# A scan and a feed-forward network in one Trainium2 kernel: first unit's decays ahead of other prelude products, weight-decoding passes placed by step, and seven-product groups in another order

## The chip, the cores and the metric

The kernel runs on one core of a Trainium2 chip. The metric is the device time of one execution in microseconds (us), lower is better. Engines are named as in the profile: PE is TensorE's matmul pipe (PEld its weight loads), DVE is VectorE, ACT is ScalarE, POOL is GpSimd, SP is SyncE (SPq when it issues transfers).

## What is computed

The reference is a chunked linear-attention scan followed by a two-layer network without biases:

```python
log_a = np.log(np.clip(a, 1e-06, 1.0))          # a: 4 x 8 x 768
for each chunk:                                  # x: 4 x 8 x 768 x 32; B, C: 4 x 8 x 768 x 16
    cum = np.cumsum(la, axis=-1)
    L = np.exp(cum[..., :, None] - cum[..., None, :]) * causal
    y = (C @ B.T * L) @ x + (C @ state) * np.exp(cum)
    state = exp(sum(la)) * state + sum over j of B_j x_j * exp(cum_last - cum_j)
h = y.reshape(3072, 256) @ w_in                  # w_in: 256 x 2048
out = np.maximum(0.01 * h, h) @ w_out            # w_out: 2048 x 256
```

Everything is float32. The kernel takes the scan in chunks of 96 positions, which gives the same values.

## The kernel before

**Units of the scan.** A unit u is one chunk of one batch row with its 8 heads; there are 8 chunks of 4 batch rows, 32 units, in the order u = 4 * chunk + batch. Each unit needs a tile `lt` of decays (112 x 8 x 96), made in one of three ways. Units 0 and 1 (`DIRECT`) get theirs from two matmul groups: `decay_mask` writes the causal mask, `decay_direct` (L242) adds the sums, and `decay_of` (L272) takes the exponential on ACT. Units 2 to 15 use one matmul group, `decay_pe` (L261), on the operands `dl` and `dr`, into which `decay_load` brings split row sums by two transfers (L250, L253) from `parts_d` in HBM; `fill_slots` (L187) fills the constant rows. Units from 16 on use broadcast rows: a transfer (L279), a subtraction on POOL (`decay_sub`, L284), an exponential (L292) and a triangle select on POOL (L293). Then `scores` (L317, or L407 for two units at a time) multiplies C by B, DVE multiplies the scores into `lt` (L322 or L420), `unit_products` (L344, L353) makes the unit's output and next state, ACT copies the state (`stage`, L377) and the high half `xh` (L382), POOL spreads the state into the next chunk's `xs` (L380), and DVE subtracts the low half `xl` (L387). `state_decay` (L299) scales a chunk's B operand on POOL. Two groups, one for each unit, run behind each other in a loop of ten iterations u = 0 to 9 (`FIRST_UNITS`); iteration u issues `decay_pe(u + 2)`, `scores(u + 1)` and the products of unit u. Iteration 9 also issues the scores and multiplies of units 10 and 11 and the first network step. The other units come in pairs between network steps (`PAIR`, `STACKED_AT`, `STACKED_OUT`), by `pair_block` or `pair_now`.

**Weights.** There are 16 slices f of 128 hidden columns. Slice f arrives as 64-bit floats in `raw` (L96, 512 KB, three buffers) and is decoded: `decode_abs` on ACT (L441), then *passes* on DVE in a fixed queue: hold (L446), shift (L452), sign (L459), low (L466). After low, `defer` notes `decode_high` on ACT (L472, writes `wh`), `decode_abs` of slice f + 1, and for slices 0 to 3 the remainder `wl` on POOL (`rest_pool`, L512); for later slices the remainder is one more DVE pass (`decode_rest`, L479). What is deferred is issued by the next `settle`, which the loop calls once in each iteration or step (with `late=True` an entry waits one iteration more). `decode(n)` issues the next n passes. In `before` the prelude issues two passes, iterations 1 to 9 without 3 issue one each, and each network step issues `PASSES` = 2.

**Network steps.** There are six tiles t of 512 tokens. Tiles 0 to 3 go by steps s = (t, f) in the order of `CELLS`, 64 steps; a *cell* is a run of steps of one tile. `ffn_in(s)` is six matmuls of 512 columns (L550) into `hp`, of which there are two buffers; ACT makes `gh` (L557) and applies the activation in place (L560), DVE makes `gl` (L563) and so frees `hp`. `ffn_out(s)` (L574, six matmuls), `LAG` = 3 steps later, adds into the two output banks; at a cell's last step the banks are emptied by ACT and DVE (L586, L588) or, with an earlier partial result, by two DVE additions (L582). The next cell's first `ffn_out` needs the emptied banks, and its step is held back one step for that.

**Tiles 4 and 5** are done together at the end (`two_tiles`), with seven products in place of eight for each pair p of slices, eight periods p. One period issues on PE: products into the banks A, B and C, a slot, `product(A, False, a12, ...)`, `product(B, False, s3, ...)`, a slot, `product(B, False, a22, ...)`, `product(C, False, s4, ...)`, and two slots. A product is three matmuls (L792); a slot is one earlier output group, six matmuls (L811, or L574 for the last steps of tile 3). On DVE: u2 = B + kept (L865), u3 = B + kept (L872), c22 = C + u3 (L873), c21 (L879), c12 (L880) and four `low` subtractions (L824); `kept` is ACT's copy of A. `sums` (L743, L752) and `sums_split` (L758) prepare the next period's weight sums on POOL. `product(B, ..., s3)` has to wait until u2 has read B, and the products after the second slot wait for c22.

**Order.** The schedule is manual: each engine runs its instructions in the order in which the code issues them.

Of the kernel before, what the change touches and what calls it, by code (L numbers as in the profile page):

```python
# [18 lines left out]
Q = 96  # L19
NC = S // Q  # L20
QE = Q + N
# [5 lines left out]
TS = 512  # L27
NT = NTOK // TS
B_COLS = NB * QE
LAG = 3  # L30
WARM = 6
WARM2 = 2
RAWS = 3
SHIFT = 448
# [20 lines left out]
LAST_OUT = 54  # L55
COMBINE = 56

PASSES = 2
KD = Q + 3 * NH + 3
MAG_MIN = float(np.uint32(0x38000000).view(np.float32))  # L60
MAG_MAX = float(np.uint32(0x47EFFFFF).view(np.float32))
# [3 lines left out]
def scan_ffn(ctx: ExitStack, tc: tile.TileContext, a_l, b_l, c_l, bn_l, x_l, w_l, out_l):  # L65
# [112 lines left out]
    def fill_first():  # L178
        nc.vector.tensor_copy(dr[:Q, 0], later.unsqueeze(1).to_broadcast([Q, NH, Q]))
# [64 lines left out]
                start=False, stop=True,  # L244
            )

    def decay_load(u, n):
        p, b = u * NH, (u - DIRECT) % SLOTS
        rows = parts_d[p:p + n * NH]
        nc.sync.dma_start(  # L250
            dl[Q:Q + 3 * NH, b:b + n, :Q], rows.rearrange("(u h) t i -> (h t) u i", h=NH)
        )
        nc.sync.dma_start(  # L253
            dr[Q + 3 * NH:KD, b:b + n].rearrange("t b h i -> t (b h) i"),
            rows.rearrange("r t i -> t r i"),
        )
# [336 lines left out]
    with tc.tile_pool(name="ps_d", bufs=2, space=PSUM, reuse_waits="tile") as ps_d:  # L593

        def free_tile():
            return ps_d.tile([128, 2, TS], F32, name="pd")

        nc.vector.tensor_scalar(
            out=la, in0=la, scalar1=1e-6, scalar2=1.0, op0=ALU.max, op1=ALU.min,
        )  # L600
        nc.scalar.activation(la, la, AF.Ln)
        pds = [free_tile() for _ in range(2)]
        second = score_tile()
        for u in range(DIRECT):
            fill_reach(u)
        nc.gpsimd.memset(ccs[1], 0.0)
        nc.vector.memset(dl[Q:], 1.0)
        nc.vector.memset(dl[Q:Q + 3 * NH, :, Q:], 0.0)
        fill_first()
        prow = first[:, 0, :Q]  # L610
        sum_rows(prow, 0)
        split_sums(prow)
        nc.sync.dma_start(parts_d, parts)
        fetch_w(0)
        decay_load(DIRECT, 2)
        decay_load(DIRECT + 2, SLOTS - 2)
        columns(erev, after, AF.Exp, second[:, 0])
        fill_less()
        for u in range(DIRECT):
            decay_mask(pds[u])  # L620
        keep_warm(second[:, 1], WARM2)
        state_decay(0)
        nc.scalar.copy(dl[:Q], upto_b.unsqueeze(1).to_broadcast([Q, SLOTS, QE]))
        fill_slots(1, SLOTS // 2)
        fill_slots(SLOTS // 2, SLOTS)
        decay_direct(0, pds[0])
        decay_of(0, pds[0])
        decode_abs(0)
        fetch_bc(1)
        fetch_bn(1)  # L630
        fetch_x(1)
        fetch_w(1)
        scores(0)
        decode(2)
        decay_direct(1, pds[1])
        decay_of(1, pds[1])
        for u in range(FIRST_UNITS):
            v = u + 2
            if u:
                decay_pe(v, free_tile())  # L640
            if u == 0:
                rest = unit_out(u, free_tile())
                rest()
            if u + 1 < FIRST_UNITS:
                scores(u + 1, int(0 < u < 4))
            else:
                pair_now((), (u + 1, u + 2))
                settle()
                pg = ctx.enter_context(tc.tile_pool(name="pg", bufs=LAG + 2))
                ffn_in(0, free_tile()[:, 0])  # L650
            if u:
                rest = unit_out(u, free_tile())
                rest()
            else:
                pd = free_tile()
                keep_warm(pd[:, 0], WARM2)
                decay_pe(v, pd)
            c, b = divmod(u, NB)
            if c + 2 <= 3:
                if b == 0 and c:  # L660
                    alloc_x(c + 2)
                    fetch_x(c + 2)
                if b == 2:
                    fetch_bc(c + 2)
                if b == 3:
                    fetch_bn(c + 2)
            if u == 3:
                fetch_x(2)
            if u == 4:
                fetch_w(2)  # L670
            if b == 2 and c < 2:
                state_decay(c + 1)
            if u > 7:
                fetch_more()
            if u:
                settle(late=True)
                if u != 3:
                    decode(1)
        ffn_act(0)
        ffn_low(0)  # L680

# [112 lines left out]
                skip_group_check=True,  # L794
            )

    def keep_out(t, m, op, half):
        ob = pob.tile([128, TS], F32, name=f"ob{m}")
        if half:
            nc.scalar.copy(ob[:, :TS // 2], op[:, :TS // 2])  # L800
            nc.vector.tensor_copy(ob[:, TS // 2:], op[:, TS // 2:])
        elif m == 0:
            nc.scalar.copy(ob, op)
        else:
            nc.vector.tensor_copy(ob, op)
        nc.sync.dma_start(out_l[m, :, t * TS:(t + 1) * TS], ob)

    def two_out(f, t, gh, gl, first, last):
        for m in range(2):
            for i, (half, x) in enumerate(((0, gh), (1, gh), (0, gl))):  # L810
                nc.tensor.matmul(  # L811
                    outs[t][m], lhsT=w_half[half][:, f, DM + m * 128:DM + (m + 1) * 128], rhs=x,
                    start=first and i == 0, stop=last and i == 2,
                )
        if last:
            for m in range(2):
                keep_out(t, m, outs[t][m], t == NT - 1 and m == 1)

    def act_split(h, gh, in_place):
        nc.scalar.activation(gh, h, AF.Prelu, alpha=0.01)  # L820
# [10 lines left out]
    def two_tiles(queue, pair, rhs):  # L831
# [9 lines left out]
        def slot():  # L841
            if queue:
                f = queue.popleft()
                f()
                if f is opens:
                    slot()

        for p in range(NP):
            f1, f2 = 2 * p, 2 * p + 1
            k1, k2 = slice(0, 128), slice(128, 256)  # L850
# [12 lines left out]
            product(C, True, s1, rhs["t1"])  # L863
            nc.scalar.copy(kept, A)
            nc.vector.tensor_tensor(out=u2, in0=B, in1=kept, op=ALU.add)  # L865
            if p + 1 < NP:
                sums(p + 1)
            slot()
            product(A, False, a12, rhs["21"])
            act_split(A, g["11"][0], A)  # L870
            product(B, False, s3, rhs["t3"])
            nc.vector.tensor_tensor(out=u3, in0=B, in1=kept, op=ALU.add)  # L872
            nc.vector.tensor_tensor(out=c22, in0=C, in1=u3, op=ALU.add)  # L873
            low(g["11"][1], A, g["11"][0])
# [9 lines left out]
            act_split(c21, g["21"][0], c21)  # L884
            low(g["21"][1], c21, g["21"][0])
            act_split(c12, g["12"][0], c12)
            low(g["12"][1], c12, g["12"][0])
            slot()
            slot()
            order = ("11", "21", "22", "12") if p == NP - 1 else ("11", "22", "21", "12")  # L890
# [10 lines left out]
    for s in range(total):  # L901
# [11 lines left out]
        settle()  # L913
        if late:
            late[1](0)
        if s:
            ffn_low(s)
        if late:
            late[1](1)
        late = None  # L920
        if s in stacked_at:
            u = stacked_at[s]
# [2 lines left out]
            for rest in rests:  # L925
                rest()
            late = (u + 1, mults)
        if s in pair_at:
            pair_now(*pair_at[s])
        decode(PASSES)  # L930
        if s == COMBINE:
            open_two()
            sums(0)
# [7 lines left out]
        if s == HELD_OUT:  # L941
            open_outs_pool()
        elif rested or not outs_due or steps[outs_due[0]] not in firsts or outs_due[0] == 0:
            while outs_due:
                ffn_out(outs_due.popleft())
            rested = False
        else:
            rested = True
    for _ in combining:
        pass  # L950
    assert not outs_due
# [42 lines left out]
```

## Time and profile before

| | us |
|---|---|
| median of three runs (lowest to highest) | 324.87 (323.07 to 325.5) |
| the profiled execution, its own time | 324.14 |
| its span, first to last instruction | 322.4 |
| PE busy, of the span | 311.1 |
| DVE busy | 213.4 |
| ACT busy | 181.4 |
| POOL busy | 132.5 |

The profiled execution's time is 1.74 us above its span; that part lies outside the instructions. PE's busy time overlaps between pipelined matmuls (a 512-column matmul shows about 390 ns, and they start 227 ns apart), so 96% is not a measure of what is left. The chain of waits follows the work that ended last backwards and is the better guide: where a row of it is not PE's, PE stood still.

### The profile page before, as it was taken

Reading aid. Unit: us, or ns where it says so; the run is one execution under the profiler, and the core shown is the slowest. Engines: PE = TensorE matmul, PEld = TensorE weight load, DVE = VectorE, ACT = ScalarE, POOL = GpSimd, SP = SyncE. Lnnn points to the kernel's source line nnn. Section 1 sums busy time; section 2 is a strip of 40 time slices with the busy share of each in tenths; the row PEclk is TensorE's granted clock in tenths of the full one; section 3 lists DMA queues with packets and bytes.
Section 4 is the critical chain, followed back from the end, with each engine's and each line's share of the span. In section 5 each row is a group of like instructions: output and inputs, shape, how many; then the busy total and the mean of one; then the engine's idle time right before and its main releaser. Section 6 shows DMA issues by size and latency. Waiting matters only on the chain.

```text
span 322.4 us, 6284 instructions
## 1 busy us (share of the span) xinstructions
PE 311.1 (96%) x2407; PEld 244.9 (76%) x2407; DVE 213.4 (66%) x349; ACT 181.4 (56%) x354; POOL 132.5 (41%) x216
## 2 busy tenths in 40 slices
PE   8999989999998999999999999999999999999995
PEld 4567768788886888788888877888877778777873
DVE  6788895797889797952634452296387577657561
ACT  5677775857575555545363534574366445644551
POOL 6388672613454443523434520070064356435100
PEclk9999999999999999999999999999999999999999
DMA  6777641462529240330213101000000000000003
GB/s 193 229 237 268 181 153 65 150 199 75 144 69 276 70 152 0 118 101 2 88 47 107 65 1 67 0 2 0 0 33 35 0 0 0 2 0 2 0 2 130
DMA packets 11722, 26.29 MB, mean 82 GB/s; under 512 B 2380, under 2 KB 4652, under 8 KB 11692
## 3 DMA queue, kind: packets, MB, share of 16 engines
q1 hardware_dynamic: 11692, 25.89, 25.3%
q8 instruction: 19, 0.31, 0.4%
q14 instruction: 11, 0.09, 0.1%
HBM read 22.57 MB, written 3.32 MB: 80 GB/s over the span
## 4 chain that ended last, share of the span: by engine, by line
PE 83%; DVE 8%; ACT 3%; issue 3%; DMA 2%; SPq 0%; ACTq 0%
PE op L574 26%; PE hp L550 24%; PE sc L792 9%; PE sc L811 6%; PE op L811 4%; PE hp L792 3%; PE sc L407 3%; PE sc L344 3%; DVE c L873 2%; DVE u L872 2%; PE sc L317 1%; PE pd L344 1%; PE pd L261 1%; DMA raw<-w_l 1%; DVE gl L563 1%
## 5 line engine op out<-in xcount | busy, mean ns | idle before, releaser
L563 DVE TENSOR_TENSOR gl<-hp,gh 128x512 fp32r<-128x512 f32 x63 | 43.4, 689 | 58.6 <-ACT hp L560 58.3
L557 ACT ACTIVATE gh<-hp 128x512 fp32r<-128x512 f32 x63 | 37.6, 597 | 63.7 <-PE hp L550 63.7
L574 PE MATMUL op<-gh,wh 128*128 128x512 f32 x128 | 51.0, 398 | 1.1 <-DVE ob L582 1.1
L550 PE MATMUL hp<-xh,wh 128*128 128x512 f32 x126 | 49.8, 395 | 0.4 <-DVE gl L563 0.4
L574 PE MATMUL op<-gh,wl 128*128 128x512 f32 x128 | 49.9, 390 | 0.0
L574 PE MATMUL op<-gl,wh 128*128 128x512 f32 x128 | 49.9, 390 | 0.0
L550 PE MATMUL hp<-xh,wl 128*128 128x512 f32 x126 | 49.1, 389 | 0.0
L550 PE MATMUL hp<-xl,wh 128*128 128x512 f32 x126 | 49.0, 389 | 0.0
L380 POOL COPY xs<-stage 16x64 f32<-16x64 f32 x112 | 31.6, 282 | 31.4 <-ACT stage L377 26.9
L758 POOL TENSOR_TENSOR sl<-s,sh 128x512 fp32r<-128x512 f32 x8 | 10.4, 1296 | 73.1 <-ACT sh L757 73.1
L293 POOL TENSOR_SCALAR_AFFINE_SELECT lt<-lt 96x768 f32<-96x768 f32 x16 | 15.1, 943 | 55.8 <-ACT lt L292 55.8
L560 ACT ACTIVATE hp<-hp 128x512 f32<-128x512 f32 x63 | 37.4, 594 | 0.0
L574 PEld LDWEIGHTS op<-gh,wh 128*128 128x128 f32 x128 | 24.0, 188 | 8.0 <-ACT gh L557 1.7
L550 PEld LDWEIGHTS hp<-xh,wh 128*128 128x128 f32 x126 | 23.7, 188 | 6.0 <-DVE gl L563 0.9
L574 PEld LDWEIGHTS op<-gl,wh 128*128 128x128 f32 x128 | 24.0, 188 | 5.1
L574 PEld LDWEIGHTS op<-gh,wl 128*128 128x128 f32 x128 | 24.0, 188 | 4.7
L550 PEld LDWEIGHTS hp<-xl,wh 128*128 128x128 f32 x126 | 23.6, 188 | 4.9
L284 POOL TENSOR_TENSOR lt<-lt,ccol 112x768 f32<-112x768 f32 x16 | 25.9, 1620 | 3.4 <-DMA lt<-crow_d 2.7
L550 PEld LDWEIGHTS hp<-xh,wl 128*128 128x128 f32 x126 | 23.7, 188 | 4.7
L824 DVE TENSOR_TENSOR gl<-c,gh 128x512 fp32r<-128x512 f32 x24 | 24.3, 1032 | 1.4 <-ACT c L821 1.2
L420 DVE TENSOR_TENSOR lt<-sc,lt 112x384 f32<-112x384 f32 x44 | 21.6, 549 | 3.0 <-ACT xh L382 1.9
L820 ACT ACTIVATE gh<-c 128x512 fp32r<-128x512 f32 x24 | 15.0, 627 | 14.7 <-DVE c L873 9.1
(165 smaller groups left out, 609.7 us busy)
## 6 DMA issues: line engine op xcount, KB each, us to landing
raw<-w_l SPq DMA_DIRECT2D x16, 512.0 KB, 3.9
lt<-crow_d SPq DMA_DIRECT2D x16, 336.0 KB, 4.6
xs<-x_l SPq DMA_DIRECT2D x8, 384.0 KB
out_l<-ob SPq DMA_DIRECT2D x12, 256.0 KB, 2.0
bn<-bn_l SPq DMA_DIRECT2D x8, 231.0 KB, 3.4
bt<-b_l SPq DMA_DIRECT2D x8, 224.0 KB, 4.7
cc<-c_l SPq DMA_DIRECT2D x16, 96.0 KB, 3.9
la<-a_l SPq DMA_DIRECT2D x1, 96.0 KB
```

What stands on the lines that cost most here:

```text
L284: nc.gpsimd.tensor_tensor(out=lts[u], in0=lts[u], in1=ccol[:, u * NH:(u + 1) * NH].unsqueeze(2).to_broadcast([QE, NH, Q]), op=ALU.subtract,)
L293: nc.gpsimd.affine_select(out=lt[:Q], in_=lt[:Q], pattern=[[0, NH], [1, Q]], compare_op=ALU.is_ge, fill=0.0, base=0, channel_multiplier=-1,)
L380: nc.gpsimd.tensor_copy(to[:, :, hh], stage[hh * D:hh * D + N])
L420: nc.vector.tensor_tensor(out=heads, in0=spaces[half][:QE, :, 2 * Q * e:2 * Q * (e + 1)], in1=heads, op=ALU.mult,)
L550: nc.tensor.matmul(hp, lhsT=w_half[half][:, f, k * 128:(k + 1) * 128], rhs=x[t][:, k, :], start=(n == 0), stop=(n == 5),)
L557: nc.scalar.activation(ghs[s], hp, AF.Prelu, alpha=0.01)
L560: nc.scalar.activation(hps[s], hps[s], AF.Prelu, alpha=0.01)
L563: nc.vector.tensor_tensor(out=gls[s], in0=hps.pop(s), in1=ghs[s], op=ALU.subtract)
L574: nc.tensor.matmul(op, lhsT=w_half[half][:, f, DM + m * 128:DM + (m + 1) * 128], rhs=x, start=(first and i == 0), stop=(last and i == 2),)
L792: nc.tensor.matmul(bank, lhsT=w[h], rhs=x[g], start=start and i == 0, stop=i == 2, skip_group_check=True,)
L811: nc.tensor.matmul(outs[t][m], lhsT=w_half[half][:, f, DM + m * 128:DM + (m + 1) * 128], rhs=x, start=first and i == 0, stop=last and i == 2,)
L824: nc.vector.tensor_tensor(out=gl, in0=g, in1=gh, op=ALU.subtract)
```

## The change

- *Prelude.* Three warming matmuls (`WARM`) instead of six; the two masks are issued straight after them, before the row sums, and the later two warming matmuls are gone. `decay_direct(0)` and its exponential come right after the first column sums; then half the constant rows of `dr`, the scores of unit 0, `decay_direct(1)`, the copy into `dl`, the two row loads, and the exponential of unit 1, then the other half of the rows. The first load's second transfer (the rows of `dr`) is issued by ScalarE instead of SP.
- *Weights.* `fetch_w(1)` moves from the prelude to iteration 2, `fetch_w(2)` from iteration 4 to 6; `decode_abs(0)` moves from the prelude to iteration 1.
- *Passes.* Iterations 2 to 9 issue `LEAD` passes. Steps issue `EARLY` (0 to 3), none in `BUSY`, three in `LIGHT`, otherwise two; in steps 1 and 3 two more stand between the two multiplies of a unit. `ffn_low` of these steps moves behind the second multiply.
- *Step 4.* The block of units 14 and 15 moves from before the passes to the end of the step, behind the output groups.
- *Seven-product groups.* `product(B, False, s3, ...)` goes ahead of `product(A, False, a12, ...)`; the `low` of c12 is issued one period later, after u2.
- *Last outputs.* Tile 5's second half is copied whole by ACT and its first half by DVE; before, the second half was shared between ACT and DVE and the first went to ACT.

Where the first passes stand (f is the slice):

| | before | after |
|---|---|---|
| prelude | hold 0, shift 0 | none |
| iterations 1 to 9 | sign 0; low 0; none; hold 1; shift 1; sign 1; low 1; hold 2; shift 2 | none; hold 0 and shift 0; sign 0; low 0; none; hold 1 and shift 1; sign 1; low 1; hold 2 |
| steps 0 to 3 | sign 2, low 2; hold 3, shift 3; sign 3, low 3; hold 4, shift 4 | none; shift 2, sign 2, low 2; none; hold 3, shift 3, sign 3, low 3 |

```diff
-WARM = 6
+WARM = 3
-PASSES = 2
+LEAD = (2, 1, 1, 0, 2, 1, 1, 1)
+EARLY = (0, 1, 0, 2)
+BUSY = (17, 21, 25, 30, 34, 38, 42, 46, 50)
+LIGHT = (9, 11, 13, 14, 16)
...
-    def decay_load(u, n):
+    def decay_load(u, n, eng=nc.sync):
...
-        nc.sync.dma_start(
+        eng.dma_start(
             dr[Q + 3 * NH:KD, b:b + n].rearrange("t b h i -> t (b h) i"),
...
         fill_first()
+        for u in range(DIRECT):
+            decay_mask(pds[u])
         prow = first[:, 0, :Q]
         sum_rows(prow, 0)
         split_sums(prow)
         nc.sync.dma_start(parts_d, parts)
         fetch_w(0)
-        decay_load(DIRECT, 2)
-        decay_load(DIRECT + 2, SLOTS - 2)
         columns(erev, after, AF.Exp, second[:, 0])
         fill_less()
-        for u in range(DIRECT):
-            decay_mask(pds[u])
-        keep_warm(second[:, 1], WARM2)
         state_decay(0)
-        nc.scalar.copy(dl[:Q], upto_b.unsqueeze(1).to_broadcast([Q, SLOTS, QE]))
-        fill_slots(1, SLOTS // 2)
-        fill_slots(SLOTS // 2, SLOTS)
         decay_direct(0, pds[0])
         decay_of(0, pds[0])
-        decode_abs(0)
+        fill_slots(1, SLOTS // 2)
+        scores(0)
+        decay_direct(1, pds[1])
+        nc.scalar.copy(dl[:Q], upto_b.unsqueeze(1).to_broadcast([Q, SLOTS, QE]))
+        decay_load(DIRECT, 2, nc.scalar)
+        decay_load(DIRECT + 2, SLOTS - 2)
+        decay_of(1, pds[1])
+        fill_slots(SLOTS // 2, SLOTS)
         fetch_bc(1)
         fetch_bn(1)
         fetch_x(1)
-        fetch_w(1)
-        scores(0)
-        decode(2)
-        decay_direct(1, pds[1])
-        decay_of(1, pds[1])
...
-                if u != 3:
-                    decode(1)
+            if u == 1:
+                decode_abs(0)
+            if u > 1:
+                decode(LEAD[u - 2])
...
+        if m == 0 and t != NT - 1:
+            nc.scalar.copy(ob, op)
+        elif t != NT - 1:
+            nc.vector.tensor_copy(ob, op)
         elif m == 0:
+            nc.vector.tensor_copy(ob, op)
+        else:
             nc.scalar.copy(ob, op)
...
             nc.vector.tensor_tensor(out=u2, in0=B, in1=kept, op=ALU.add)
+            if low_due:
+                low(*low_due.pop())
             if p + 1 < NP:
                 sums(p + 1)
             slot()
+            product(B, False, s3, rhs["t3"])
             product(A, False, a12, rhs["21"])
             act_split(A, g["11"][0], A)
-            product(B, False, s3, rhs["t3"])
...
             act_split(c12, g["12"][0], c12)
-            low(g["12"][1], c12, g["12"][0])
+            low_due.append((g["12"][1], c12, g["12"][0]))
+            if p + 1 == NP:
+                low(*low_due.pop())
...
         if late:
             late[1](0)
+            decode(2)
+            late[1](1)
         if s:
             ffn_low(s)
-        if late:
-            late[1](1)
...
-        if s in pair_at:
+        if s in pair_at and s != STACKED_OUT:
             pair_now(*pair_at[s])
-        decode(PASSES)
+        decode(EARLY[s] if s < len(EARLY) else 0 if s in BUSY else 3 if s in LIGHT else 2)
...
+        if s == STACKED_OUT:
+            pair_now(*pair_at[s])
```

More of the change, by code (lines that the diff above doesn't have):

```diff
@@ L664, in scan_ffn @@
                     fetch_bc(c + 2)
+                    if c == 0:
+                        fetch_w(1)
                 if b == 3:
@@ L668, in scan_ffn @@
                 fetch_x(2)
-            if u == 4:
+            if u == 6:
                 fetch_w(2)
@@ L795, in product, with keep_out @@
             )
-    def keep_out(t, m, op, half):
+    def keep_out(t, m, op):
         ob = pob.tile([128, TS], F32, name=f"ob{m}")
-        if half:
-            nc.scalar.copy(ob[:, :TS // 2], op[:, :TS // 2])
-            nc.vector.tensor_copy(ob[:, TS // 2:], op[:, TS // 2:])
+        if m == 0 and t != NT - 1:
+            nc.scalar.copy(ob, op)
+        elif t != NT - 1:
+            nc.vector.tensor_copy(ob, op)
         elif m == 0:
+            nc.vector.tensor_copy(ob, op)
+        else:
             nc.scalar.copy(ob, op)
-        else:
-            nc.vector.tensor_copy(ob, op)
         nc.sync.dma_start(out_l[m, :, t * TS:(t + 1) * TS], ob)
@@ L816, in two_out @@
             for m in range(2):
-                keep_out(t, m, outs[t][m], t == NT - 1 and m == 1)
+                keep_out(t, m, outs[t][m])
     def act_split(h, gh, in_place):
@@ L846, in slot @@
                     slot()
+        low_due = []
         for p in range(NP):
```

## The prediction

> **What bounds the kernel now.** I read the page first, then the chain of waits from end to end, then PE's list of waits, and last the timeline around each place where the chain leaves PE.
>
> ```profile
> span 322.4 us, 6284 instructions
> ...
> PE 83%; DVE 8%; ACT 3%; issue 3%; DMA 2%; SPq 0%; ACTq 0%
> ```
>
> ```profile
> PE sc L344 <- DVE lt L420: 1.9, 2, 1.4
> ...
> PE op L574 <- DVE ob L582: 1.1, 1, 1.1
> PE pd L261 <- ACT lt L272: 0.8, 1, 0.8
> ...
> PE hp L550 <- DVE gl L563: 0.4, 1, 0.4
> ```
>
> PE is the bound; what can be gained is the time in which it stands. The list (total us, times, longest) names four places outside the end: steps 2 and 4 (L420: 0.5 and 1.4), a cell's end (L582: 1.1), iteration 5 (L272: 0.8) and one late `gl` (0.4). The seven-product part waits a little in each of its periods:
>
> ```profile
> 253.22 0.69 PE sc L792 x3
> 253.94 0.70 DVE u L872
> 254.67 0.70 DVE c L873
> 255.41 1.67 PE sc L792 x6
> ...
> 258.47 1.36 PE op L811 x6
> ...
> 263.91 0.69 PE sc L792 x3
> ```
>
> Six 512-column matmuls take 1.36 us, 0.227 each. From s3 at 253.22 to the next s3 at 263.91 is one period, 10.69 us, for 45 matmuls (seven products of 3, four slots of 6), which is 10.20. The 0.49 between them comes from s3, u3 and c22 in a row: the slot beside them covers 1.36 of their 1.5 and latencies, and the restart costs the rest.
>
> **Prelude, 1.7 us earlier.**
>
> ```profile
> 5.57 1.46 PE L242 MATMUL pd<-lt,after 96*112 96x384 f32 x4
> ...
> 5.95 2.45 DVE L187 COPY dr<-dr 120x2304 bf16<-120x2304 bf16 x2 [0.29 <-ACT dr L183]
> ...
> 7.80 0.37 SPq L250 DMA_DIRECT2D dl<-parts_d  x1
> ...
> 9.46 0.68 ACT L441 ACTIVATE w<-raw 128x512 f32<-128x512 f32 x1 [1.59 <-DMA raw<-w_l]
> ...
> 10.04 0.79 ACT L272 ACTIVATE lt<-pd 112x768 f32<-112x768 f32 x1
> ...
> 11.46 1.01 DVE L322 TENSOR_TENSOR lt<-sc,lt 112x384 f32<-112x384 f32 x2
> ...
> 13.04 0.54 PE L344 MATMUL pd<-lt,xs 96*32 96x96 f32 x16
> ```
>
> Here the wait is on ACT: unit 1's exponential (10.04) stands behind `decode_abs(0)`, which waits 1.59 for the first weights. After the change, unit 0's matmuls start about 1.1 earlier (4.5), its exponential ends near 6.8, when ACT is free of the `dr` rows. DVE fills half the rows (1.2 of the 2.45), multiplies unit 0 until 8.2 and fills the rest until 9.5. ACT copies into `dl`, issues the row transfer once `parts_d` has landed (SP could issue at 7.80; 0.3 for the issue, as a bound 0 to 0.6) and runs unit 1's exponential from 8.1 to 8.9. DVE is then the later one: `xl` of unit 0 until 9.9, multiply of unit 1 from 9.9 and not 11.46. PE's products of unit 1 go from 13.04 to about 11.3: 1.7. The loads are the bound below: should their small packets, which sit behind the weights that ended at 9.46, land only at 10.5, it is 1.0. Three warming matmuls and the masks fill the same time as six did, so the row sums start as before: nothing. Moving `fetch_w(1)` and `fetch_w(2)` costs nothing: iterations later than their issue by 4 us use them.
>
> **Iterations 1 to 5, 0.3 us gained.** `decode_abs(0)` (0.68) now stands between `xh` and the next exponential on ACT, which has some 0.3 of room there: 0.4 lost. Two passes in iteration 2, where there was one, lose 0.2. `decode_high(0)` and `decode_abs(1)` leave iteration 4, and with them the wait of 0.8 (0.9 with its restart): gained.
>
> **Iteration 6, 2.8 us lost.** The same two ACT instructions, the POOL remainder and now two passes come in iteration 6, which has a POOL instruction that iteration 4 had not: `state_decay(2)`.
>
> ```profile
> 15.57 0.21 ACT L377 COPY stage<-pd 128x64 f32<-128x64 f32 x1 [0.51 <-PE pd L353]
> ...
> 17.45 1.06 POOL L299 TENSOR_TENSOR bn<-bn,erev 112x512 f32<-112x512 f32 x1
> ...
> 19.32 0.21 ACT L377 COPY stage<-pd 128x64 f32<-128x64 f32 x1 [0.59 <-PE pd L353]
> ...
> 20.90 0.43 DVE L446 TENSOR_SCALAR w<-w 128x512 f32<-128x512 f32 x1 [0.76 <-ACT w L441]
> 20.91 1.54 POOL L512 TENSOR_TENSOR wl<-w,wh 128x512 fp32r<-128x512 f32 x1
> ...
> 24.30 0.68 DVE L459 SCALAR_TENSOR_TENSOR w<-raw,w 128x512 uint32<-128x512 uint32 x1
> ```
>
> ```profile
> 126.52 1.23 POOL L293 TENSOR_SCALAR_AFFINE_SELECT lt<-lt 96x768 f32<-96x768 f32 x1 [4.97 <-ACT lt L292]
> ...
> 127.05 2.69 DVE L466 SCALAR_TENSOR_TENSOR w<-raw,w 128x512 uint32<-128x512 uint32 x1
> ...
> 127.73 1.46 POOL L284 TENSOR_TENSOR lt<-lt,ccol 112x768 f32<-112x768 f32 x1
> ```
>
> The second fence shows how a pass behaves against POOL: L466, issued at 127.05 while L293 ran, did not get in between L293 and L284 and ended at 129.74, after both. In the first, POOL's L512 came 0.01 behind hold (L446) and lasted 1.54. So they exclude each other, and a waiting engine goes first when the other has a gap. Counted from T, the start of `stage` of unit 6: hold 1 comes at T + 1.58 (20.90 less 19.32), L299 at T + 1.88 (17.45 less 15.57). Shift 1 needs hold 1 and so leaves a gap at T + 2.0; L299 takes it (1.06), L512 follows at once (1.3), and shift 1 ends near T + 4.6. The multiply of unit 8, queued behind it on DVE, started in before at T + 1.34; it starts at T + 4.6 now. DVE then works without a pause through iterations 7 to 9 (two multiplies 1.0 each, three `xl` 0.36, sign 1 and low 1 at 0.7 as at 24.30, the multiplies of units 10 and 11 at 1.95, hold 2, `gl(0)`), and PE's `decay_pe(12)`, which waits for `gl(0)`, comes 2.8 later by this count than at before's distance from T.
>
> The Trainium skill (SBUF — State Buffer, "SBUF: two separate sides") says that DVE instructions with two SBUF inputs or in a two-port mode, and GpSimd's, share one pair of ports, held by whichever starts first for the whole instruction. It speaks against putting two passes beside POOL work, and the trace agrees (2.69 for L466). It does not say who is next: if shift 1 gets in between L299 and L512, only 1.1 is lost at first; that is the first rival.
>
> **Steps 0 to 6, 0.1 us gained.** Without passes in step 0 and with `gl` behind the second multiply, the multiplies of units 13 and 15 come 0.6 and 0.5 earlier, so the wait of 0.5 in step 2 goes; in step 4 PE runs two output groups (2.72) in place of its wait of 1.4. But both are given back. ACT's `decode_high(2)`, issued in step 2, waits for low 2, which DVE reaches only after shift 2, sign 2, two multiplies (1.0 each) and `gl(1)`; the unit copies and the exponential of unit 14 stand behind it, and `decay_pe(15)` comes 0.2 later than before. Low 3 now ends step 3 and not step 2: ACT's high, then POOL's remainder, which slice 3's step 5 needs:
>
> ```profile
> 44.29 1.28 POOL L512 TENSOR_TENSOR wl<-w,wh 128x512 fp32r<-128x512 f32 x1 [0.90 <-ACT wh L472]
> 44.86 0.54 PE L344 MATMUL sc<-lt,xs 112*32 112x96 f32 x16 [1.36 <-DVE lt L420]
> ```
>
> Before, that remainder was ready at 45.57, with 3 us to spare. After, low 3 ends near 46.8 on the same scale, the remainder near 48.8, and step 5's second matmul, which could start at 47.6, waits for it. Net 0.1, with 1.9 (no wait returns) and -0.6 as its ends.
>
> **Ends of cells, 1.6 us gained.**
>
> ```profile
> 101.32 1.79 POOL L284 TENSOR_TENSOR lt<-lt,ccol 112x768 f32<-112x768 f32 x1 [2.18 <-DMA lt<-crow_d]
> ...
> 101.70 1.96 DVE L459 SCALAR_TENSOR_TENSOR w<-raw,w 128x512 uint32<-128x512 uint32 x1
> ...
> 104.41 0.47 PE L574 MATMUL op<-gh,wh 128*128 128x512 f32 x1 [1.05 <-DVE ob L582]
> ```
>
> The additions that empty the banks in step 21 stand behind sign 11, which is slow beside L284. With no pass in step 21 they run at 101.2 and PE does not wait: 1.2 with the restart. The other wait (0.4, some 0.6 with its restart) is the 2.69 of L466 above, low 14 ahead of `gl(30)`. There hold 14 and shift 14 stand now, which can lose to the same two POOL instructions, but are shorter: 0.4 of 0.6. The three-pass steps lie where PE has output groups to run. Bounds 0 and 1.8.
>
> **Seven-product groups, 4.2 us gained.** With a12 behind s3, PE has 0.68 + 1.36 to do while u3 and c22 run, about 1.5: the 0.49 goes, eight times 3.9. What must now be early is u2, before s3:
>
> ```profile
> 258.33 3.37 DVE L824 TENSOR_TENSOR gl<-c,gh 128x512 fp32r<-128x512 f32 x3
> 258.53 1.75 POOL L743 TENSOR_TENSOR w<-wh,wl 128x512 f32<-128x512 f32 x1
> ...
> 261.96 0.69 DVE L865 TENSOR_TENSOR u<-sc,kept 128x512 f32<-128x512 f32 x1 [0.27 <-issue]
> ...
> 263.07 0.39 PE L792 MATMUL hp<-xh,wh 128*128 128x512 f32 x1
> ```
>
> u2 ended at 262.65; s3 would start where a12 does, at 263.07: 0.4 of cover. The third `low` (0.95 of the 3.37) leaves u2's front, so u2 moves up by up to 0.7. In the second period u2 stood behind an output copy, and s3 waited about 0.6 on it; of that 0.3 to 0.5 goes. Sum 4.2, bounds 3.0 and 4.4.
>
> **Tail, 0.2 us gained.**
>
> ```profile
> 317.98 0.59 ACT L803 COPY ob<-op 128x512 f32<-128x512 f32 x1 [1.45 <-PE op L811]
> ...
> 318.66 0.37 ACT L800 COPY ob<-op 128x256 f32<-128x256 f32 x1
> 319.06 0.42 DVE L801 COPY ob<-op 128x256 f32<-128x256 f32 x1 [1.81 <-ACT ob L800]
> ```
>
> The halves ran one behind the other until 319.48. A whole ACT copy, 0.59 as at 317.98, ends at 319.25. Bounds 0 and 0.3.
>
> **Sum.** 1.7 + 0.3 - 2.8 + 0.1 + 1.6 + 4.2 + 0.2 = 5.3. The profiled execution took 324.14, its span and 1.74 around it: 318.8. The shown median, 324.87, is 0.7 above that execution and the lowest run 1.1 below; the sum rests on the profiled one.
>
> **Rivals.** (1) Shift 1 gets in before L512, or sign 1 rather than shift 1 loses: `decay_pe(12)` loses 1.5 in place of 2.8, 317.5. For it: hold 1 came ahead of L512 at 20.90; against: L466 was passed over at 127.73. (2) POOL is behind or ahead and nothing collides: only the two ACT instructions cost, 0.6, and 316.6. Against: 0.3 between the two arrivals. (3) The passes make new waits in the steps: with low 15 in step 35 (32 before) more passes meet L284, and the 1.6 comes back as waits, with 0.7 more at step 5: 321.1. (4) Slower: DVE becomes the bound in the three-pass steps 9, 11, 13, 14 and 16. A step then has `gl` and three passes, 2.5 us, and with one pass held off by L284 as at 101.70 (1.3 more) 3.8, against 2.72 of PE's; `hp` comes free late and PE waits 1.0 in each, 5.0, on top of rival 3's 2.3: 324.14 - 5.3 + 7.3 = 326.1. It decides from a wait of 0.6 in each. For it: how long a pass is held off; against: `hp` has two buffers, so that a late `gl` is wanted a step later, and steps 10, 12 and 15 have two passes. (5) The prelude's gain is not there since the loads land late, 1.0 in place of 1.7: 319.5, inside the forecast's own spread.
>
> **Chances.** Forecast 0.47 (with 5), rival 1 0.2, rival 2 0.13, rival 3 0.17, rival 4 0.03. One per cent of the time before, 3.2 us, is about what a measurement of this kernel can tell from no change, so 321.6 is the border: rival 3 lies at it, and I give it half. Faster 0.88, within 0.1, slower 0.02. The range leaves out half of rival 3 and all of 4 above and the best of 2 below: 315.6 to 321.3.
>
> **What would show it.** Right: no row of u3 and c22 in the chain between 230 and 305, and 10.2 from s3 to s3; no wait on L582; unit 1's products near 11.3; a shift 1 of over 2 us near L299 and L512 in iteration 6; a wait of PE's step 5 for L512. The forecast is wrong if the first network step comes earlier than before by over 0.5 us (rival 1 or 2; by the forecast it comes about 0.8 later), if periods still take 10.6, or if PE waits for `gl` or `ob` in steps 9 to 40 for over 1 us (rival 3, and from 5 us rival 4).

## The result, and the profile after

The changed kernel took 325.68 us in the median of nine executions (319.15 to 327.12), the kernel before 324.54 in nine of the same comparison. The nine lie in three groups: one at 319.15, three at 321.6 to 322.2, five at 325.7 to 327.1. The comparison leaves the last five out as disturbed, which gives a ratio of 0.99 (95%: 0.9857 to 0.9942); since the upper group turns out to come from the clock at the kernel's start, all nine are kept here and told apart below. By the median of all nine the change gains nothing. One of the nine, 319.15, lies in the forecast's range of 315.6 to 321.3. The profiled execution is one of the middle group, 321.56, with 1.76 around its span: 2.6 less than before's 324.14, where 5.3 had been forecast.

The page of the kernel after; `PEclk` is the granted clock of TensorE in 40 slices of 8 us:

```profile
span 319.8 us, 6252 instructions
...
PEclk9995999999999999999999999999999999999999
...
PE 89%; DVE 6%; ACT 2%; issue 2%; POOL 0%; DVEq 0%; POOLq 0%
```

The share of PE in the chain rose from 83% to 89%, and there is something that the page of before did not have: a slice at half the clock (the 5). PE's waits (us in total, times, longest):

```profile
PE sc L320 <- DVE lt L325: 2.2, 1, 2.2
...
PE hp L553 <- POOL wl L515: 0.7, 1, 0.7
PE pd L264 <- ACT lt L275: 0.7, 1, 0.7
PE hp L553 <- DVE gl L566: 0.4, 1, 0.4
PE px__874 L264 <- ACT lt L275: 0.4, 1, 0.4
PE sc L795 <- DVE u L870: 0.3, 1, 0.3
```

The waits of 0.5 and 1.4 in steps 2 and 4, the 1.1 at a cell's end and the many small ones of the seven-product part are gone. The 0.8 of iteration 5, behind two ACT instructions, stands in iteration 6 now, as 0.7 (L264). New are 2.2 in iteration 6, 0.7 in step 5, 0.4 for a late `gl` in step 10 (the one in step 32 is gone) and 0.4 ahead of a `decay_pe`. Between the two profiles PE gained and lost, by starts of the same instructions:

| stretch | before | after | gained | forecast |
|---|---|---|---|---|
| to unit 1's products | 13.04 | 11.65 | +1.4 | +1.7 |
| from there to unit 6's `stage` | 10.52 | 10.06 | +0.5 | +0.3 |
| from there to step 6 | 26.68 | 30.81 | -4.1 | -2.7 |
| step 6 to step 63 | 175.31 | 174.35 | +1.0 | +1.6 |
| step 63 to the end of the span | 96.88 | 92.97 | +3.9 | +4.4 |

The prelude, in PE's timeline and in that of all engines (start, us, engine, line):

```profile
4.95 1.46 PE L245 MATMUL pd<-lt,after 96*112 96x384 f32 x4
6.34 0.59 PE L320 MATMUL sc<-cc,bt 32*112 32x192 f32 x8
6.86 1.54 PE L245 MATMUL pd<-lt,after 96*112 96x384 f32 x4
```

```profile
8.44 0.81 ACT L275 ACTIVATE lt<-pd 112x768 f32<-112x768 f32 x1 [0.22 <-PE pd L245]
8.62 0.95 DVE L190 COPY dr<-dr 120x3072 bf16<-120x3072 bf16 x1
...
10.07 1.01 DVE L325 TENSOR_TENSOR lt<-sc,lt 112x384 f32<-112x384 f32 x2
...
11.65 0.54 PE L347 MATMUL pd<-lt,xs 96*32 96x96 f32 x16
```

Unit 1's exponential ran at 8.44 and not at 10.04, DVE multiplied at 10.07 and not at 11.46: the two steps of the forecast, each within 0.4. Iteration 6:

```profile
21.71 0.21 ACT L380 COPY stage<-pd 128x64 f32<-128x64 f32 x1 [0.58 <-PE pd L356]
...
23.12 1.06 POOL L302 TENSOR_TENSOR bn<-bn,erev 112x512 f32<-112x512 f32 x1
...
23.29 2.40 DVE L449 TENSOR_SCALAR w<-w 128x512 f32<-128x512 f32 x1 [0.75 <-ACT w L444]
...
24.00 0.48 PE L264 MATMUL pd<-dr,dl 123*112 123x384 bf16 x2 [0.66 <-ACT lt L275]
...
24.14 1.26 POOL L515 TENSOR_TENSOR wl<-w,wh 128x512 fp32r<-128x512 f32 x1
...
25.72 0.43 DVE L455 TENSOR_SCALAR w<-w 128x512 uint32<-128x512 uint32 x1
26.06 1.01 DVE L325 TENSOR_TENSOR lt<-sc,lt 112x384 f32<-112x384 f32 x2
26.66 1.45 PE L320 MATMUL sc<-cc,bt 32*112 32x192 f32 x8 [2.18 <-DVE lt L325]
...
28.04 0.87 PE L347 MATMUL pd<-lt,xs 112*32 112x96 f32 x16
```

Hold 1 (L449, normally 0.43) came 0.17 behind `state_decay(2)` (L302), was passed over when the POOL remainder (L515) followed it, and lasted 2.40. The multiply of unit 8 stood behind it, and PE waited 2.18. Ahead of that it had waited 0.66 for the exponential (L275) behind ACT's two weight instructions. The last two rows show the other thing: eight L320 took 1.45, and sixteen L347 0.87 in place of 0.54. The windows (us, then busy time and instructions of PE, its weight loads, DVE, ACT, POOL, then the granted clock, DMA share, GB/s):

```profile
4.80:25.30 20.50, 18.89 (x361) 11.31 (x359) 17.25 (x35) 15.74 (x34) 13.39 (x34) 1.00 0.85 235
25.30:32.20 6.90, 5.54 (x60) 3.88 (x61) 5.15 (x12) 2.40 (x6) 3.39 (x10) 0.51 0.67 194
32.20:230.00 197.80, 196.18 (x1598) 158.75 (x1597) 132.92 (x218) 113.60 (x230) 78.69 (x126) 1.00 0.30 90
```

From 25.35, within the wait, to 32.18 TensorE was granted half its clock. Nothing in the forecast stood for that. Steps 5 and 6, then step 10:

```profile
49.96 1.27 POOL L515 TENSOR_TENSOR wl<-w,wh 128x512 fp32r<-128x512 f32 x1 [3.01 <-ACT wh L475]
...
51.28 0.50 PE L553 MATMUL hp<-xh,wl 128*128 128x512 f32 x1 [0.69 <-POOL wl L515]
...
53.15 0.19 PEld L553 LDWEIGHTS hp<-xl,wh 128*128 128x128 f32 x1 [0.44 <-DVE xl L390]
```

```profile
60.39 1.23 POOL L296 TENSOR_SCALAR_AFFINE_SELECT lt<-lt 96x768 f32<-96x768 f32 x1 [3.21 <-ACT lt L295]
...
60.81 2.81 DVE L462 SCALAR_TENSOR_TENSOR w<-raw,w 128x512 uint32<-128x512 uint32 x1
...
61.60 1.47 POOL L287 TENSOR_TENSOR lt<-lt,ccol 112x768 f32<-112x768 f32 x1
...
63.54 0.68 DVE L566 TENSOR_TENSOR gl<-hp,gh 128x512 fp32r<-128x512 f32 x1
...
64.27 0.50 PE L553 MATMUL hp<-xh,wh 128*128 128x512 f32 x1 [0.39 <-DVE gl L566]
```

Slice 3's remainder is late for step 5, as forecast, and an `xl` for step 6. Sign 6 (L462), which the new distribution put beside L296 and L287, takes 2.81, and a `gl` is late by it: one wait of this kind was taken away late in the steps and one came early. The seven-product part, in the chain:

```profile
245.33 1.36 PE sc L795 x6
...
255.53 1.36 PE sc L795 x6
...
265.73 1.36 PE sc L795 x6
```

10.20 a period, the count of its matmuls, in place of 10.69, and from 244 to 310 the chain has no row but PE's.

### The profile page after: what moved, and what is told of

Same layout as the page of the kernel before. It is cut to its first block, busy times and chain, and to the rows that moved or that the text cites. A ratio compares the mean times of both kernels' runs of the same rounds, so it can differ in the third digit from the quotient of the medians.

```text
span 319.8 us, 6252 instructions
## 1 busy us (share of the span) xinstructions
PE 310.2 (97%) x2402; PEld 246.3 (77%) x2402; DVE 214.4 (67%) x349; ACT 180.8 (57%) x353; POOL 130.9 (41%) x216
## 3 DMA queue, kind: packets, MB, share of 16 engines
q1 hardware_dynamic: 11641, 25.88, 26.8%
## 4 chain that ended last, share of the span: by engine, by line
PE 89%; DVE 6%; ACT 2%; issue 2%; POOL 0%; DVEq 0%; POOLq 0%
PE op L577 26%; PE hp L553 25%; PE sc L795 9%; PE op L815 7%; PE sc L815 6%; PE hp L795 3%; PE sc L410 3%; PE sc L347 2%; PE sc L320 2%; PE pd L347 1%; DVE w L462 1%; PE pd L264 1%; DVE lt L423 1%; DVE w L449 1%; PE sc L127 1%
## 5 line engine op out<-in xcount | busy, mean ns | idle before, releaser
L560 ACT ACTIVATE gh<-hp 128x512 fp32r<-128x512 f32 x63 | 37.6, 597 | 63.6 <-PE hp L553 63.4
L383 POOL COPY xs<-stage 16x64 f32<-16x64 f32 x112 | 30.5, 272 | 30.5 <-ACT stage L380 25.3
L296 POOL TENSOR_SCALAR_AFFINE_SELECT lt<-lt 96x768 f32<-96x768 f32 x16 | 15.7, 982 | 47.4 <-ACT lt L295 47.4
L287 POOL TENSOR_TENSOR lt<-lt,ccol 112x768 f32<-112x768 f32 x16 | 26.7, 1671 | 10.0 <-DMA lt<-crow_d 9.2
L828 DVE TENSOR_TENSOR gl<-c,gh 128x512 fp32r<-128x512 f32 x24 | 23.2, 968 | 0.9 <-ACT c L825 0.7
L824 ACT ACTIVATE gh<-hp 128x512 fp32r<-128x512 f32 x8 | 4.8, 599 | 27.1 <-PE hp L795 27.1
```

The costliest lines, as they stand in the source:

```text
L287: nc.gpsimd.tensor_tensor(out=lts[u], in0=lts[u], in1=ccol[:, u * NH:(u + 1) * NH].unsqueeze(2).to_broadcast([QE, NH, Q]), op=ALU.subtract,)
L296: nc.gpsimd.affine_select(out=lt[:Q], in_=lt[:Q], pattern=[[0, NH], [1, Q]], compare_op=ALU.is_ge, fill=0.0, base=0, channel_multiplier=-1,)
L383: nc.gpsimd.tensor_copy(to[:, :, hh], stage[hh * D:hh * D + N])
L560: nc.scalar.activation(ghs[s], hp, AF.Prelu, alpha=0.01)
L828: nc.vector.tensor_tensor(out=gl, in0=g, in1=gh, op=ALU.subtract)
```

## The experiments

The theory after the result: the two POOL instructions hold hold 1 off and PE waits 2.2; the wait lets the granted clock fall, which costs about as much again; and in the upper group the clock rises late in the prelude, since three warming matmuls do not always bring it up. The rivals: the loss of iteration 6 is the two ACT instructions and not the collision; the steps' new places of passes make the loss; the groups come from elsewhere.

### The scaling one iteration earlier

```diff
-            if b == 2 and c < 2:
+            if b == 2 - c and c < 2:
                 state_decay(c + 1)
```

> The changed kernel, with the scaling of chunk 2's B operand on POOL issued in iteration 5 and no longer in iteration 6, so that it doesn't stand next to the remainder of slice 0. Theory A (the two POOL instructions in a row hold off hold 1, PE then stands 2.2 us and runs at half clock for 6.8 us after it): hold 1 takes 0.43, no wait of over 1 us on the multiply, granted clock 0.99 or above with no half-clock stretch near 25 to 32 us, first network step near 27.6 in place of 31.5, and about 4 us less than the changed kernel's profiled execution: 317.5. Theory B (what is lost lies in the steps, and the wait in iteration 6 only moves an idle time that would come anyway at step 0): first network step earlier, but the wait for gl(0) or step 5 grows by as much, 320.5 to 321.5.

Measured: 322.53 in the median of ten (317.85 to 325.18), ratio 0.9887 (0.984 to 0.9935). Two of ten came to 317.85 and 318.82, near what was expected, the others to 321.8 or more. The profiled one is of the latter, 321.81, and shows both halves:

```profile
25.96 0.21 ACT L380 COPY stage<-pd 128x64 f32<-128x64 f32 x1 [0.58 <-PE pd L356]
...
27.53 0.43 DVE L449 TENSOR_SCALAR w<-w 128x512 f32<-128x512 f32 x1 [0.75 <-ACT w L444]
27.99 0.43 DVE L455 TENSOR_SCALAR w<-w 128x512 uint32<-128x512 uint32 x1
...
28.14 1.42 POOL L515 TENSOR_TENSOR wl<-w,wh 128x512 fp32r<-128x512 f32 x1
...
28.94 1.05 PE L320 MATMUL sc<-cc,bt 32*112 32x192 f32 x8 [0.20 <-DVE lt L325]
```

The collision is gone: hold and shift take 0.43 each, PE waits 0.20, and from `stage` of unit 6 to step 6 (at 52.8) it is 26.8 us, near before's 26.7 and not 30.8: collision and half clock together cost 4.0. Up to step 0 alone it is 6.1, against 5.3 in before and 9.7 in after, so 0.8 stays lost without the collision: PE still waits 0.5 behind the two ACT instructions (28.25) and the 0.20. The steps up to 6 give 0.6 of it back. But `stage` of unit 6 itself comes at 25.96, not 21.71. The prelude of the same profile:

```profile
5.03 2.77 PE L245 MATMUL pd<-lt,after 96*112 96x384 f32 x4
7.72 1.00 PE L320 MATMUL sc<-cc,bt 32*112 32x192 f32 x8
8.65 2.90 PE L245 MATMUL pd<-lt,after 96*112 96x384 f32 x4
```

The same four matmuls that took 1.46 and 1.54 take 2.77 and 2.90. The clock's first full record in this trace is at 14.57, in after's at 4.87: 4.25 us lost ahead of iteration 6, 4.0 won in it. Ahead of the first record the page's clock row and the windows show full clock all the same (1.00 from 0 to 14 us here); there the matmuls' own durations are what tells.

### The changed kernel profiled twice more

Unchanged, to see an execution of the upper group.

> The changed kernel once more, unchanged, for a second profile: its times come in groups near 322 and near 326.5, and only one of the first group has a profile. If the upper group is that of executions whose full clock comes late in the prelude (theory), then a profile at 325 to 328 has its first clock record only after 8 us, decay_direct(1) at L245 in 2.5 us or more in place of 1.54, the first network step at 34 us or later in place of 31.5, and from step 6 on the same distances as before (step 63 at 174.4 behind step 6). If the upper group comes from somewhere else (rival: a slower stretch in the steps or in the seven-product groups), the first step is at 31.5 also there and the 4.5 us lie behind it. With a time near 322 the profile repeats the first one and tells nothing new.

> As for the run before it, the same kernel: five of nine executions lay in the upper group, so one of two profiles is likely to show it. The same two readings apply.

Measured: 327.07 and 327.08. Both are of the upper group, and PE's timeline of the first is that of the experiment above:

```profile
5.01 2.77 PE L245 MATMUL pd<-lt,after 96*112 96x384 f32 x4
...
8.64 2.90 PE L245 MATMUL pd<-lt,after 96*112 96x384 f32 x4
```

The first full record is at 15.37 and 17.15, the first step at 35.6 and 36.8 (31.5 in the first profile), step 6 at 58.0 in both (52.5), and from there to step 63 it is 174.4 in both, as in the first. So the upper group is the late clock, and nothing behind step 6 is part of it. That is shown for the two of its seven executions that were traced; the other five lie with them by their times.

### Six warming matmuls in the changed kernel

```diff
-WARM = 3
+WARM = 6
...
-        for u in range(DIRECT):
-            decay_mask(pds[u])
...
         columns(erev, after, AF.Exp, second[:, 0])
+        for u in range(DIRECT):
+            decay_mask(pds[u])
```

> The changed kernel with six warming matmuls again and the two masks behind the row and column sums; the two POOL instructions still stand together in iteration 6. Theory A2 (with three warmers PE is granted full speed at 5 us in some executions and at 14.6 us in others, which is the 4 to 5 us between 321.6 and 326.5): full clock at 4 to 6 us, no execution over 324, all within 319 to 322.5, and in iteration 6 the held-off hold 1 as before. Rival A3 (the two groups of times come from iteration 6, where a half-clock stretch may follow the wait or not): still two groups, some executions at 325 to 327.

Measured: 322.21 in the median of ten, ratio 0.9939 (0.9911 to 0.9967). Eight lie at 321.1 to 323.3, two at 327.0: the upper group is there in 2 of 10, against 7 of 11 with three warming matmuls. The collision is untouched (hold 1 takes 2.39, PE waits 2.2), and half the clock follows from 28.39 to 31.80, 3.4 us in place of 6.8.

### Three warming matmuls in the kernel before

```diff
-WARM = 6
+WARM = 3
...
-        keep_warm(second[:, 1], WARM2)
```

> The kernel before with three warming matmuls and without the two later ones, nothing else. A2: full clock late, at 8 us or after, in some or all executions, which then take 3 to 5 us more: 327 to 329.5, others at 324. A3: no difference, 323 to 326.

Measured: 324.73 in the median of ten, ratio 1.0048 (0.9994 to 1.0102). Six lie at 323.6 to 324.8, four at 328.1 to 329.0. The profiled one, 324.2, got the full clock at 8.21, against 4.01 in before, and its first step came 0.6 later. Whether fewer warming matmuls alone make before's upper group more frequent is not shown: with six, before itself came to 327.9 or more in 4 of the 19 executions of the same comparison, and no execution of either one's upper group was traced. The frequency also moves with something outside the kernel, since before came there in none of 28 executions of the first two comparisons and in 6 of 30 of the last two. Within one comparison the clearest count is the first experiment's: 8 of 10 at 321.8 or more, against none of before's 19 at 327.9 or more. These two differ in the whole prelude and not in the warming matmuls alone.

### Both together

Six warming matmuls, and the scaling one iteration earlier.

> As the kernel before this one, and the scaling of chunk 2 moved to iteration 5. A2 with A: full clock at 4 to 6 us, no wait of over 1 us in iterations 1 to 9, first network step at 27.5 to 28.3, 316.5 to 318 in all executions. If the moved scaling only helped because PE was slow in the first 14 us: wait for it in another place, 319 or more.

Measured: 318.8, 319.21, 322.85 and 324.13; the median 321.03, the ratio 0.9894 (0.98 to 0.9988). The profiled one is the 324.13, with the first full record at 16.42: six do not exclude the late clock. In it PE has no wait of 2.2, and `stage` of unit 6 to step 6 takes 27.6.

### The seven-product part alone

The kernel before with the product s3 ahead of a12, the late `low` and the last copies.

```diff
+            product(B, False, s3, rhs["t3"])
             product(A, False, a12, rhs["21"])
             act_split(A, g["11"][0], A)
-            product(B, False, s3, rhs["t3"])
...
-            low(g["12"][1], c12, g["12"][0])
+            low_due.append((g["12"][1], c12, g["12"][0]))
...
```

> The kernel before with only the seven-product order, the deferred low and the last copies. Both theories: no wait between u3, c22 and the next products, 10.2 us from s3 to s3, 3.9 to 4.2 us less from 228 us on, 320.2 (ratio 0.987). If a late u2 or a slow low takes the place of the wait: 322 to 324.

Measured: 319.57, 320.64, 319.41 and 324.14, the median 320.1, ratio 0.9884 (0.982 to 0.9948). From step 63 to the end of the span it is 92.8 us, 96.9 in before and 93.0 in after: 4.0 of gain, with the tail, and all of after's. Alone it is as good as the whole change in its lower groups (ratio 0.99), and better than the whole change's median.

### The steps' passes alone

The kernel before with the passes placed by step, two between the two multiplies of a unit, and step 4's block behind the output groups. Its loop had issued one pass more by step 0 than after's, so that each pass stands one place earlier than there.

```diff
-        decode(PASSES)
+        decode(EARLY[s] if s < len(EARLY) else 0 if s in BUSY else 3 if s in LIGHT else 2)
...
```

> The kernel before with only the passes of the network steps and the block of units 14 and 15 in their new places. Theory A: the waits of 0.5 and 1.4 us in steps 2 and 4 and the one of 1.1 at the cell's end go, one of 0.5 us comes in step 10: 1 to 2 us less, 322.3 to 323.3. Theory B (the steps lose): 324.5 or more.

Measured: 325.21 in the median of ten, ratio 1.0013 (0.999 to 1.0036): nothing. Its waits:

```profile
PE hp L552 <- DVE gl L565: 2.4, 4, 0.9
...
PE hp L552 <- POOL wl L514: 0.4, 1, 0.4
```

The waits of steps 2 and 4 and of the cell's end went (0.5, 1.4, 1.1), and four of `hp` for a late `gl` came, 2.4 in place of 0.4, with the remainder's 0.4. Four passes between 47 and 67 us take 1.6 to 2.7 beside L514, L286 and L295. Step 6 comes 0.7 earlier than in before, and from there to step 63 it is 2.0 longer, where after is 1.0 shorter. That is what the forecast's rival 3 tells of, and more. The steps' code is that of after, so the one place is the likely reason; the weights also arrive at other times, so it is not shown alone.

### The prelude and the first loop alone

The kernel before with after's code from the first sums to the end of iteration 9, `decay_load` and `LEAD`; the steps stay as in before.

> The kernel before with only the prelude's order, the ScalarE row transfer and the passes and weight loads of the first ten iterations; two passes in every step as before. Theory A: unit 1's products at 11.7, then the 2.2 us wait in iteration 6 and a half-clock stretch, first network step near 31.5 and the whole 1.5 to 3 us slower than before, 325.5 to 327. Theory B: the prelude's gain reaches the steps, 322 to 323.5.

Measured: 330.55 in the profiled execution, the lowest of six, 334.87 in the median, ratio 1.0312 (1.0289 to 1.0336). That is worse than either theory gave. Its waits:

```profile
PE sc L318 <- DVE lt L323: 2.2, 1, 2.2
PE op L575 <- ACT wh L473: 1.9, 1, 1.9
PE sc L345 <- DVE lt L421: 1.9, 2, 1.4
PE op L575 <- DVE ob L589: 1.3, 1, 1.3
```

Step 6 starts 3.2 later than in before, with the collision's 2.2 and half a clock from 28.47 to 31.88. Step 14 is 3.9 behind, step 21 7.6: two of the waits are weights that come late (L473) and a cell's end (L589). One pass fewer is issued ahead of the steps and the steps are as they were, so the likely reason is that the weights' queue is late where it had been just in time. PE also waits 0.9 for the loads of the split row sums (`dl` from `parts_d`) near 11 us, which is the forecast's rival 5. The two halves of the change belong together, so this run prices neither. The five others, at 334.5 to 337.6, have no trace; that they are late-clock executions is likely by their distance of 4.0 and more, and not shown.

### The version with the passes moved

Both together as above, and two passes moved: step 2 has the two that step 3 had, and step 10 takes step 9's third.

```diff
-EARLY = (0, 1, 0, 2)
+EARLY = (0, 1, 2, 0)
-LIGHT = (9, 11, 13, 14, 16)
+LIGHT = (10, 11, 13, 14, 16)
```

> As the second kernel of these, with hold 3 and shift 3 in step 2 and sign 3 and low 3 between the multiplies of step 3, and three passes in step 10 and not in step 9. If low 3 is what step 5 waits for: PE's wait of 0.7 us on slice 3's remainder goes and the one of 0.4 in step 11 as well, 1 to 1.5 us less than the second kernel, 315.5 to 316.5. If DVE is what counts there: the wait moves to the multiplies of units 14 and 15, same time as the second kernel.

Measured: 317.85, 317.44, 322.62 and 322.26; the median 320.05, ratio 0.9813 (0.9759 to 0.9867). PE's waits of the profiled 317.85:

```profile
PE sc L410 <- DVE lt L325: 0.4, 1, 0.4
PE hp L553 <- DVE gl L566: 0.4, 1, 0.4
```

Neither 2.2 nor 0.7 is in its list, the clock is full from 4.97 on, and step 6 starts at 48.9 (50.2 in before, 52.5 in after). The late `gl` stayed: another sign pass was held off for 2.80. Two of its four executions are the lowest of all; the other two are 322.26 and 322.62. By the ratio it is below before, by the median of four it is level with the seven-product part alone (320.1).

### Ten warming matmuls in that version

```diff
-WARM = 6
+WARM = 10
```

> The version with six warming matmuls, the early scaling and the passes moved, now with ten warming matmuls. The four more take 4 x 0.43 = 1.7 us at half clock (six took 2.74 from start to end, three 1.46), and the row sums start later by that: 319.5 in place of 317.6 where the full clock comes early in both. If what makes the clock come late is too little PE work ahead of the row sums (theory), no or almost no execution shows the late group (some 4.5 us higher, 324), where six warmers had 10 of 79 and three had 22 of 35: of ten, one at most. If the late group is a matter of chance that the warmers do not touch (rival), one to three of ten lie near 324, and the median is 319.5 or above.

Measured, in six executions and not ten: 318.95, 319.54, 319.91, 322.53, 322.6 and 323.76; ratio 0.9862 (0.9803 to 0.9921), not better than six. The profiled one, 322.53, has the full clock from 4.24, but three waits that the version with six had not:

```profile
PE op L577 <- DVE ob L591: 1.3, 1, 1.3
...
PE sc L320 <- DVE lt L325: 1.0, 1, 1.0
...
PE pd L264 <- DMA dr<-parts_d: 0.8, 1, 0.8
```

It also has half the clock from 28.13 to 31.55. Arrivals had moved, and hold 1 and L302 met once more (1.18 in place of 0.43). Whether more warming matmuls end the late clock can't be told: of six executions with a chance like the 2 of 10 above, one would have been late, and none is plainly so.

## Why the prediction was right, and where it was wrong

**The parts** were right: the chain is PE's, the prelude's 1.4, iterations 1 to 5 with 0.5 and the end's 3.9 came as worked out, within 0.5 each, and iteration 6 lost to two POOL instructions in a row. **The direction** holds for the four lower executions of nine only; five are slower than before's median. The one at 319.15 lies 0.4 from the forecast, but has no trace. That the profiled one, at 321.56, lies near rival 3's 321.1 is luck: it lost most in iteration 6, by the collision and the clock, and not by waits in the steps. Rivals 1 and 2 are out, by hold 1's 2.40; rival 4 is out, since no step between 9 and 40 waits over 0.4; rival 5's late loads did not show in after's profile.

**The step that failed** is the sentence "Three warming matmuls and the masks fill the same time as six did, so the row sums start as before: nothing." The row sums did start as before (L220 at 3.6), but the start of the full clock was left out. 7 of 11 executions are about 5 us longer, and in the two of them that were traced the full clock came at 15 and 17 us and not at 5, with 5.5 lost by step 6. The counts point to the number of warming matmuls (7 of 11 with three and 2 of 10 with six in after; 4 of 10 and 4 of 19 in before), but they are small, after's two are of different comparisons, and with six the late clock came too (16.42). So the late clock is shown as the cause of the upper group; that fewer warming matmuls make it more frequent is likely and not shown. The Trainium skill (TensorE: Matmul & The Clock Gate, "Part 1: The HAM clock gate") has the gate judge windows of 3.4 us that run on whatever the kernel does, so that where the kernel starts in a window is chance. The traces agree in this: every stretch of clock between two changes is a multiple of 3.413 us (20.48, 6.83, 23.9, 13.65), and the same kernel has its first full record at 4.87, 15.37 and 17.15. That it is the phase which decides was not tried.

**Iteration 6, forecast -2.8 with -2.7 up to step 6, measured -4.1.** The collision is as told, except that hold 1 and not shift 1 lost: the multiply came 4.35 behind `stage`, where 4.6 had been forecast. PE's two waits, 0.66 and 2.18, add up to the forecast's 2.8; the collision's part is 2.0 (2.2, and 0.2 without it). The term that the forecast had at nothing is the half clock behind it, about 2.0 by difference: with the collision gone both go, 4.0. With 3.4 us of half clock in place of 6.8 the stretch was 3.4 longer than in before (30.1 from `stage` of unit 6 to step 6). The 319.15 is the one execution of after with a mean clock of 1.0. The Trainium skill (TensorE: Matmul & The Clock Gate, "HAM oscillation") tells of waits for transfers longer than one window, over 3.4 us, that bring the clock down. Here shorter ones did: in the window ahead of the fall, 21.93 to 25.35, PE's longest gaps are 0.66 and the first 0.87 of the 2.18; the measurement decides.

**Ends of cells, forecast 1.6, measured 1.0.** The waits on L582 and the late 0.4 went, and gave 1.3 and 0.8 by the distances of the steps around them (1.2 and 0.6 in the forecast). The mis-sized part is what comes in their place, for which the forecast had 0.2: sign 6, held off by L296 and L287 for 2.81, took 0.8 of PE around step 10, and the late `xl` in step 6 took 0.3. The 0.7 in step 5 is as forecast. In the experiment with the passes one place off the new waits took all of it, so this term rested on places that were not worked out pass by pass.

**Seven-product groups and tail, forecast 4.4, measured 3.9.** The periods shown are at their 10.20. The second period keeps a wait of 0.3 for u2 (242.30), which stands behind an output copy; it was 0.5 in before, and the forecast had 0.3 to 0.5 of its cost go.

## What to carry to other kernels

A change to the matmuls that only warm, or one that opens gaps on PE, is to be costed twice: by the time itself, and by the clock that TensorE may be granted behind it. Where two POOL instructions stood in a row, a DVE instruction that couldn't run beside them and arrived in the first waited for both; moving one of the two away brought it from 2.40 back to 0.43. When a time comes in groups, profile an execution of each before a term is blamed.

## What the runs showed of the hardware

*The clock falls after less than a whole window of rest.* Counting PE's records in the window of 3.413 us ahead of each change, the clock was halved behind windows with 36, 36, 43, 54, 58 and 63% of busy time (six traces); the longest gap in each was 0.9 to 2.2 us. Once full, it kept until the tail behind all windows with 69% and more. The share alone is no border: behind four windows with 60, 60, 60 and 62% and one gap of 1.3 to 1.4 us (41.56 in before, 42.70 in the seven-product part alone, 45.53 in the prelude alone, 75.92 with ten warming matmuls) it stayed full. What else counts stays open. Behind 61 and 64% a halved clock stayed half; it came back behind a window of 100%, in one trace (15.37 above) only behind the second.

*At the start, busy time doesn't decide alone.* In the first experiment PE's records fill 96, 100, 100 and 100% of the four windows from 0.9 to 14.57, and only then is the clock full; in after one window with as much was enough. Those windows hold mostly matmuls with 96 rows and 96 or 384 columns, besides the warming ones. What the gate counts there stays open.

*A DVE instruction behind two POOL instructions waits for both*: 2.40 for 0.43 (hold 1), 2.81 for 0.68 (sign 6), in each case with the second POOL instruction starting while DVE's stood ready.
